# Reordering the opening of a fused dynamic-convolution and maxout kernel: two products in halves, and w1 cast by GpSimd's transfers

## The chip, the cores and the metric

The kernel runs on one core of a Trainium2 chip. The metric is the device time of one execution in microseconds (us); lower is better. Runs of the same kernel differ: the three runs of the kernel before lie between 410.51 and 413.79 us.

## What is computed

A dynamic convolution with seven taps feeds a two-branch maxout layer.

```python
# x: (8, 4160, 192), weight_gen: (8, 4160, 8 heads, 7 taps), float32
w = weight_gen - np.max(weight_gen, axis=-1, keepdims=True)
w = np.exp(w)
w = w / (np.sum(w, axis=-1, keepdims=True) + 1e-09)
x_pad = np.concatenate([np.zeros((B, pad, D), dtype=np.float32), x], axis=1)
...
out = np.einsum('bshk,bskhg->bshg', w, x_unf)   # 24 features a head
# then, with tokens = 33280, w1 and w2 (192, 1024), w_out (1024, 192)
h1 = x @ w1
h2 = x @ w2
g = np.maximum(h1, h2)
return (g @ w_out).astype(np.float32)
```

The kernel writes max(h1, h2) as h1 + relu(h2 - h1). So it needs the difference w2 - w1 (called wd) for the hidden layer, and the product w1 · w_out (called w10), which carries the h1 part straight to the result.

## The kernel before, in words

**Tiling.** Each of the 128 partitions holds 260 consecutive tokens, called columns here. Columns are worked in batches of 16; a batch is cut into pieces of 8, and in the first two batches into pieces of 4. For a piece, VectorE multiplies seven shifted copies of x by the softmax weights into m_t (`mul`, L208). In the first two batches TensorE then sums the seven taps and transposes at once (`sum_transpose`, L275), and ScalarE copies the result out as yt; in later batches VectorE adds the taps and a DMA transposes. `hid_tile` (L334) multiplies yt by wd, ScalarE applies Relu (`relu`, L349), `out_first` and `out_second` multiply by w10 and w_out, and `evac` copies the result for its store.

**Order.** The schedule is manual: on every engine instructions run in the order in which the code emits them, and an instruction whose data has not come holds up all behind it on its engine. Transfers issued by SyncE (SP) take one queue, those issued by GpSimd (POOL) another; POOL's loads write float32 inputs as bfloat16. `behind(first, load)` makes POOL wait for a named instruction before it issues a load.

**The opening** is the part in question, L561 to L742.

- SP's queue, in order: the weights of columns 0 to 7 (`load_wg`, L568); into xs the six columns of halo and then four columns of x (L569); the left halves of w1 and w2 for their first 128 rows (ws0E, ws1E; `load_w`, L577); the last 64 rows (ws0T, ws1T; `load_w_rest`, L584); the weights of columns 8 to 15; the right halves of ws0E and ws1E; and the weights of batch 1.
- POOL's queue: x columns 4 to 7 behind the first exponential (L655), columns 8 to 11 behind the first product (L656), 12 to 15, then w_out as wo (L658); later the first half of batch 1 behind the first Relu (L676) with its halo (L154).
- VectorE: the softmax sum and the subtraction for columns 0 to 7 (`red` L178, `shift` L188), two casts of xs (L611), the product of columns 0 to 3 (L612), the left difference of the weights (`w_diff`, L618), the difference of the last rows (L664), the product of columns 4 to 7 (L666), the right difference (L667), the sums for columns 8 to 15 and for batch 1 (L670, L672), the subtraction for columns 8 to 15 (L686), and the product of columns 8 to 11 (L689).
- TensorE: 24 matmuls that only keep it busy (`keep_warm`, L647), the tap sums of columns 0 to 3 with the first `halves_swapped` (L622) between their two halves, the second `halves_swapped`, hidden tiles 0 and 1, the tap sums of columns 4 to 7, and so on. `halves_swapped` makes the copy of wd with its partitions' halves exchanged, which ScalarE writes back into wd (L626); a hidden tile reads both forms.
- ScalarE: exponentials, logarithms and weights, a cast of the left half of ws0E to w1 (L616), the copies of wd and yt, the Relus, and after yt of columns 4 to 7 the casts of ws0T and of the right half of ws0E (L690, L691). `w1_transposed` (L631) needs these; it leads to w1t (L722), `w10_product` (L699, which also reads wo) and w10 (L713, L715).

One tap sum in `sum_transpose` reads blocks of 128 values, in which the two pairs of columns of a piece lie side by side, 64 values each; so it needs the products of both pairs.

Of the kernel before, what the change touches and what calls it, by code (L numbers as in the profile page):

```python
# [13 lines left out]
ALU = mybir.AluOpType  # L14
# [3 lines left out]
def _sub(base: bass.AP, off: int, dims):  # L18
    ap = [list(base.ap[0])] + [[int(s), int(c)] for s, c in dims]
    return dataclasses.replace(base, offset=base.offset + off, ap=ap)  # L20
# [3 lines left out]
def kernel(  # L24
# [9 lines left out]
    nc = tc.nc  # L34

    B, S, D = x.shape
    H, K = weight_gen.shape[2], weight_gen.shape[3]
    F = moe_w1.shape[1]
    P = 128
# [90 lines left out]
    def load_x(b, o, n, halo=True):  # L130

        t, at = x_at(b, o)
        load = nc.gpsimd.dma_start(  # L133
            out=t[:, at + PAD * D:at + (PAD + n) * D],
            in_=bass.AP(tensor=x.tensor, offset=actual(BATCHES[b][0] + o) * D,
                        ap=[[CPP * D, P], [1, n * D]]),
        )
        if 0 < b < NB - 1 and o == 0 and halo:
            load_halo(b)
        if "wrap" in xb_ts and t is xb_ts["wrap"]:  # L140
            nc.gpsimd.memset(t[0:1, 0:PAD * D], 0.0)
            nc.gpsimd.dma_start(
                out=t[1:P, 0:PAD * D],
                in_=bass.AP(tensor=x.tensor, offset=(CPP - PAD) * D, ap=[[CPP * D, P - 1], [1, PAD * D]]),
            )
        return load
# [11 lines left out]
    def exp_sum(b, i=0, of=1):  # L158
        if i == 0:
            e_ts[b] = pe_.tile([P, BATCHES[b][1] * WGC], FP32, name="e_t", tag="e")  # L160
        w = BATCHES[b][1] * WGC // of
        return nc.scalar.activation(out=e_ts[b][:, i * w:(i + 1) * w], in_=wg_ts[b][:, i * w:(i + 1) * w], func=AF.Exp)  # L162
# [15 lines left out]
    def red(b, i=0, of=1):  # L178
        hs, at, ap = part(b, i, of)
        nc.vector.reduce_sum(out=sums(b, hs), in_=_sub(e_ts[b], at, ap), axis=AX.X)  # L180
# [27 lines left out]
    def mul(b, o):  # L208

        n = dict(pieces(b))[o]  # L210
        t, at = x_at(b, o)
        if n == 4 and b < 2:
            m_out = _sub(m_t, K * o * D, [[64, 2], [P, K * 6], [1, 64]])
            x_in = _sub(t, at, [[2 * D, 2], [D, K], [1, 2 * D]])
        else:
            m_out = m_t[:, K * o * D:K * (o + n) * D]
            x_in = _sub(t, at, [[D, K], [1, n * D]])
        return nc.vector.tensor_tensor(  # L218
            out=m_out, in0=x_in,
            in1=_sub(en_ts[b], o * WGC * 2, [[2, K * n * H], [0, G // 2], [1, 2]]),  # L220
            op=ALU.mult,
        )

# [45 lines left out]
    def half(j):  # L269
        return slice(64 * j, 64 * j + 64)  # L270
# [4 lines left out]
    def sum_transpose(u, taps=range(K), amid=lambda: None, now=True):  # L275

        b, o, n = UNITS[u]
        assert n == 4
        yps = ps["r" if "r" in ps else "o"].tile([P, 1024], FP32, name="yps", tag="op")
        for k in range(6):  # L280
            if k == 3:
                amid()
            for t in taps:
                for r in range(2):
                    at = (K * o + t * n) * D + k * P
                    nc.tensor.matmul(  # L286
                        yps[:, r * 512 + k * 64:r * 512 + (k + 1) * 64],
                        lhsT=m_t[half(r), at:at + P], rhs=ident[half(r), half(r)],
                        start=(k == 0 and t == taps[0]), stop=(t == taps[-1]),
                        skip_group_check=True,  # L290
                    )
        def copy():
            yt = pyt.tile([P, 8 // 2 * 3 * P], BF16, name="yt", tag="yt")
            yt_of[u] = nc.scalar.copy(out=_sub(yt, 0, [[64, 2], [P, 6], [1, 64]]),  # L294
                                      in_=_sub(yps, 0, [[512, 2], [64, 6], [1, 64]]))
            yt_ts[u] = yt

        if now:
            copy()
        return copy  # L300
# [4 lines left out]
    def behind(first, load):  # L305

        tc.add_manual_dep(load.ins, first.ins.name, SYNC, reason="its place among the transfers")
# [26 lines left out]
    def hid_tile(t):  # L334


        u = TILES[t][0]
        fs, w = chunks(t)
        for f in fs:
            for s in range(3):  # L340
                for j in range(2):
                    nc.tensor.matmul(  # L342
                        hid_out(t, f, j), lhsT=wd_at(j, s, f // 4, f % 4 * P, P),
                        rhs=_sub(yt_ts[u][half(j), :], (s + j) % 3 * P, [[3 * P, w // P], [1, P]]),
                        start=(f == fs[0] and s == 0), stop=(f == fs[-1] and s == 2),
                        skip_group_check=True,
                    )

    def relu(rd, t0, n):  # L349

        (hd, at), k = hd_at[t0], rd_at[t0][1]
        relu_of[t0] = nc.scalar.activation(out=rd[:, k * 1024:(k + n) * 1024], in_=hd[:, at:at + n * 1024],  # L352
                                           func=AF.Relu)
# [126 lines left out]
    def room(g):  # L480

        t0, n = GROUPS[g]
        if "c" in ps:
            ab = ps["ab"].tile([P, 2048], FP32, name="hd2", tag="ab")
            for t in range(t0, t0 + n - 1):
                hd_at[t] = ab, (t - t0) * 1024
            hd_at[t0 + n - 1] = ps["c"].tile([P, 1024], FP32, name="hd1", tag="c"), 0
        else:
            for t in range(t0, t0 + n):
                hd_at[t] = ps["h"].tile([P, 1024], FP32, name="hdp", tag="hd"), 0  # L490
        rd = prd.tile([P, 3 * 1024], BF16, name="rd_t", tag="rd")
        for t in range(t0, t0 + n):
            rd_at[t] = (rd, t - t0)
        return rd
# [66 lines left out]
    with tc.tile_pool(name="pstage", bufs=1) as pstage:  # L561
# [4 lines left out]

        xb_ts[0] = pxb.tile([P, (16 + PAD) * D], BF16, name="xb_t", tag="xb")
        load_wg(0, nc.sync, 0, 8)  # L568
        for at, c, n in ((0, 2, PAD), (PAD, 8, 4)):  # L569
            nc.sync.dma_start(  # L570
                out=xs[:, at * D:(at + n) * D],
                in_=bass.AP(tensor=x.tensor, offset=c * D, ap=[[CPP * D, P], [1, n * D]]),
            )
# [33 lines left out]
            step(0, 0, 2)  # L607
        weights(0, 0)
        weights(0, 4)
        for at, n in ((0, PAD), (PAD, 4)):  # L610
            nc.vector.tensor_copy(out=xb_ts[0][:, at * D:(at + n) * D], in_=xs[:, at * D:(at + n) * D])  # L611
        first_mul = mul(0, 0)  # L612
        w1 = {kind: pstage.tile([P, w], BF16, name="w1" + kind)
              for kind, w in (("E", F), ("T", HF))}

        nc.scalar.copy(out=w1["E"][:, 0:HF], in_=ws["E", 0][:, 0:HF])  # L616

        def w_diff(kind, c, to):  # L618
            nc.vector.tensor_tensor(out=wd[:, to * HF:(to + 1) * HF], in0=ws[kind, 1][:, c:c + HF],
                                    in1=ws[kind, 0][:, c:c + HF], op=ALU.subtract)  # L620

        def halves_swapped(frm, bank):  # L622

            nc.tensor.matmul(bank, lhsT=ident[:, 64:64 + P], rhs=wd[:, frm * HF:(frm + 1) * HF],
                             start=True, stop=True, skip_group_check=True)
            nc.scalar.copy(out=wd[:, (frm + 3) * HF:(frm + 4) * HF], in_=bank)  # L626
# [20 lines left out]
        def keep_warm(times):  # L647

            for _ in range(times):
                nc.tensor.matmul(warm[:, 0:512], lhsT=ident[:, 0:P], rhs=_sub(ident, 0, [[0, 4], [1, P]]),  # L650
                                 start=True, stop=True, skip_group_check=True)

        keep_warm(24)
        w_diff("E", 0, 0)
        behind(first_exp, load_x(0, 4, 4))  # L655
        behind(first_mul, load_x(0, 8, 4))  # L656
        load_x(0, 12, 4)
        nc.gpsimd.dma_start(  # L658
            out=wo[:, :].rearrange("p (f d) -> p f d", d=D),
            in_=bass.AP(tensor=moe_w_out.tensor, offset=0, ap=[[D, P], [P * D, FCH], [1, D]]),  # L660
        )

        sum_transpose(0, amid=lambda: halves_swapped(0, warm[:, 512:1024]))
        w_diff("T", 0, 2)  # L664
        halves_swapped(2, warm[:, 0:512])
        mul(0, 4)  # L666
        w_diff("E", HF, 1)  # L667

        exp_sum(0, 1, 2)
        red(0, 1, 2)  # L670
        exp_sum(1)
        red(1)  # L672
        rd = room(0)
        hid_tile(0)
        relu(rd, 0, 1)
        behind(relu_of[0], load_x(1, 0, 8))  # L676
        hid_tile(1)

        def last_rows():
# [1 line left out]
            halves_swapped(1, other[:, 0:512])  # L681

        features = sum_transpose(1, amid=last_rows, now=False)
        ln(0, 1, 2)
        relu(rd, 1, 1)
        shift(0, 1, 2)  # L686
        weights(0, 8)
        features()
        mul(0, 8)  # L689
        nc.scalar.copy(out=w1["T"], in_=ws["T", 0])  # L690
        nc.scalar.copy(out=w1["E"][:, HF:F], in_=ws["E", 0][:, HF:F])  # L691
        hidden(1)
        weights(0, 12)
        ln(1)
        shift(1)
        mul(0, 12)
        tp = w1_transposed()
# [272 lines left out]
```

## Time and profile before

| what | value |
|---|---|
| median of 3 runs | 412.61 us |
| lowest and highest run | 410.51 and 413.79 us |
| the profiled execution | 413.05 us |
| its span in the trace | 411.2 us |
| mean granted TensorE clock | 0.994 |
| TensorE busy | 398.7 us, 97% of the span |
| VectorE, ScalarE, GpSimd busy | 376.0, 357.1 and 74.7 us |

The span is what the trace covers; the profiled execution took 1.85 us more than that outside it. All positions below are us from the start of the span. PE is TensorE's matmul side and PEld its weight loads, DVE is VectorE, ACT ScalarE, POOL GpSimd, SP SyncE. A name with an arrow, such as `m_t<-xb_t,en_t`, is output and inputs; L218 is line 218. Square brackets at the end of a line give the idle time of the engine ahead of it, and what ended that.

### The profile page before, as it was taken

The page shows a single profiled execution, that of the slowest core. Times are in us where ns is not written, and L with a number is a line of the kernel's source. Part 1 is how long each engine was busy: PE and PEld are TensorE (multiplying, and loading weights), DVE is VectorE, ACT ScalarE, POOL GpSimd, SP SyncE. Part 2 cuts the span into 40 slices and gives each one's busy share as a digit, 9 for nine tenths or more (in the row PEclk, how much of TensorE's full clock was granted, in tenths as well). Part 3 has the DMA queues.
Part 4 walks back from the last instruction along what each step waited for, and adds up shares of the span by engine and source line. Part 5 has one row for each costly group of instructions (what it writes and reads, how often), then busy time and mean ns, then how long its engine had stood idle before and what let it go on. Part 6 is the DMA issues. An engine that isn't in the chain of part 4 may idle for free.

```text
span 411.2 us, 16177 instructions
## 1 busy us (share of the span) xinstructions
PE 398.7 (97%) x7411; PEld 316.3 (77%) x7411; DVE 376.0 (91%) x223; ACT 357.1 (87%) x424; POOL 74.7 (18%) x105
## 2 busy tenths in 40 slices
PE   7779999999999999999999999999999999999996
PEld 2568989777777787777777777787778777777795
DVE  4889999999999999999999999999999999999500
ACT  3599989999989999898998899998999989988872
POOL 1202013122220122222202121220132221110000
PEclk9899999999999999999999999999999999999999
DMA  8947396876557874964775498478748647944413
GB/s 234 211 105 176 104 197 160 175 162 148 159 120 152 229 159 110 257 168 87 227 201 122 93 254 185 79 242 135 175 102 244 167 70 222 193 97 120 133 73 126
DMA packets 63062, 65.53 MB, mean 159 GB/s; under 512 B 47761, under 2 KB 52113, under 8 KB 62992
## 3 DMA queue, kind: packets, MB, share of 16 engines
q1 hardware_dynamic: 54320, 40.15, 35.7%
q0 software_dynamic: 8528, 24.23, 29.4%
q8 instruction: 58, 0.95, 0.9%
q10 hardware_dynamic: 144, 0.10, 0.1%
q14 instruction: 12, 0.10, 0.1%
HBM read 36.55 MB, written 25.56 MB: 151 GB/s over the span
## 4 chain that ended last, share of the span: by engine, by line
PE 91%; ACT 5%; DMA 2%; DVE 1%; issue 0%; SPq 0%; ACTq 0%; DVEq 0%
PE op_ps L382 41%; PE hd L342 38%; PE op_ps L394 8%; ACT rd_t L352 2%; PE hdp L342 2%; DMA xs<-in_x_dram 2%; PE yps L286 2%; DVE m_t L218 1%; ACT en_t L202 1%; ACT yt L294 1%; ACT w1t L722 0%; ACT xb_t L150 0%; ACT o_t L438 0%; ACT wd L626 0%; DVE xb_t L611 0%
## 5 line engine op out<-in xcount | busy, mean ns | idle before, releaser
L352 ACT ACTIVATE rd_t<-hd 128x1024 bf16<-128x1024 f32 (+1 forms) x206 | 234.5, 1187 | 26.6 <-PE hd L342 25.3
L382 PE MATMUL op_ps<-wo,rd_t 64*128 64x192 bf16 x4160 | 210.3, 243 | 0.4 <-issue 0.3
L382 PEld LDWEIGHTS <-rd_t 64*128 64x128 bf16 x4160 | 180.3, 94 | 16.6 <-issue 0.6
L218 DVE TENSOR_TENSOR m_t<-xb_t,en_t 128x10752 bf16<-128x10752 bf16 (+1 forms) x37 | 187.5, 5070 | 1.2 <-ACT en_t L202 1.1
L342 PE MATMUL hd<-yt,wd 64*128 64x512 bf16 (+1 forms) x1584 | 187.3, 360 | 0.3 <-issue 0.3
L342 PEld LDWEIGHTS <-wd 64*128 64x128 bf16 x1776 | 93.0, 94 | 44.3 <-issue 2.7
L260 POOL CAST gate<-yt 128x1 f32<-128x1 bf16 x29 | 37.2, 1284 | 261.4 <-DMA yt<-y_t 261.4
L234 DVE TENSOR_TENSOR m_t<-m_t 128x4608 bf16<-128x4608 bf16 (+1 forms) x30 | 74.1, 2470 | 0.1
L438 ACT COPY o_t<-op_ps 128x384 f32<-128x384 f32 (+1 forms) x99 | 57.4, 590 | 12.6 <-PE op_ps L382 12.5
L394 PE MATMUL op_ps<-w,yt 64*128 64x192 bf16 x780 | 55.3, 243 | 0.5 <-ACT w L715 0.4
L394 PEld LDWEIGHTS <-yt 64*128 64x128 bf16 x780 | 38.1, 94 | 17.1 <-issue 1.7
L240 DVE TENSOR_TENSOR m_t<-m_t 128x3072 bf16<-128x3072 bf16 (+1 forms) x29 | 49.9, 1722 | 0.1
L202 ACT ACTIVATE en_t<-wg_t 128x896 bf16<-128x896 f32 (+2 forms) x45 | 36.0, 823 | 0.7 <-DVE wg_t L191 0.7
L243 DVE TENSOR_TENSOR y_t<-m_t 128x1536 bf16<-128x1536 bf16 (+1 forms) x29 | 27.3, 940 | 0.5
L133 POOL DMA_DIRECT2D xb_t<-in_x_dram x34 | 18.2, 536 | 32.5 <-ACT rd_t L352 20.7
L191 DVE TENSOR_TENSOR wg_t<-wg_t,ln_t 128x280 f32<-128x280 f32 (+5 forms) x46 | 22.1, 480 | 2.0 <-ACT ln_t L186 2.0
L162 ACT ACTIVATE e_t<-wg_t 128x896 f32<-128x896 f32 (+2 forms) x18 | 16.2, 902 | 1.5 <-DMA wg_t<-in_weight_gen_dram 1.5
L180 DVE TENSOR_REDUCE s_rest<-e_t 128x64 f32<-128x448 f32 (+2 forms) x27 | 16.3, 602 | 0.3 <-ACT e_t L162 0.3
L352 ACT ACTIVATE rd_t<-hdp 128x1024 bf16<-128x1024 f32 x16 | 16.1, 1059 | 0.4 <-PE hdp L342 0.4
L342 PE MATMUL hdp<-yt,wd 64*128 64x256 bf16 x192 | 14.0, 281 | 1.0 <-ACT rd_t L352 0.6
L286 PE MATMUL yps<-ident,m_t 64*128 64x64 bf16 x636 | 11.3, 191 | 2.7 <-DVE m_t L218 2.7
L286 PEld LDWEIGHTS <-m_t 64*128 64x128 bf16 x636 | 10.6, 96 | 3.8 <-DVE m_t L218 3.2
(53 smaller groups left out, 73.6 us busy)
## 6 DMA issues: line engine op xcount, KB each, us to landing
out_dram<-o_t SPq DMA_DIRECT2D x22, 768.0 KB, 5.1
xb_t<-in_x_dram POOLq DMA_DIRECT2D x30, 384.0 KB, 5.2
out_dram<-o_t SPq DMA_DIRECT2D x20, 384.0 KB, 3.1
wg_t<-in_weight_gen_dram POOLq DMA_DIRECT2D x13, 448.0 KB, 5.7
xb_t<-xb_t POOLq DMA_DIRECT2D x15, 288.0 KB, 5.3
xb_t<-in_x_dram POOLq DMA_DIRECT2D x4, 192.0 KB, 5.1
xs<-in_x_dram SPq DMA_DIRECT2D x1, 576.0 KB, 4.5
ws0E<-in_moe_w_dram SPq DMA_DIRECT2D x2, 256.0 KB, 6.8
```

Source lines behind the costliest of these rows:

```text
L202: nc.scalar.activation(out=_sub(en_ts[b], (o * WGC + j * N * K) * 2, [[2 * N, K], [2, N], [1, 2]]), in_=_sub(wg_ts[b], (o * H + j * N) * K ...
L218: return nc.vector.tensor_tensor(out=m_out, in0=x_in, in1=_sub(en_ts[b], o * WGC * 2, [[2, K * n * H], [0, G // 2], [1, 2]]), op=ALU.mult,)
L234: nc.vector.tensor_tensor(out=taps(0, 1, 3), in0=taps(0, 1, 3), in1=taps(3, 1, 3), op=ALU.add)
L240: nc.vector.tensor_tensor(out=taps(0, 2, 2), in0=taps(0, 2, 2), in1=taps(1, 5, 2), op=ALU.add)
L243: nc.vector.tensor_tensor(out=_sub(y_ts[b], o * D, [[64, 2], [P, 3 * w // 2], [1, 64]]), in0=taps(0, 1, 1), in1=taps(2, 1, 1), op=ALU.add,)
L260: nc.gpsimd.tensor_copy(out=gate, in_=yt[:, 0:1])
L286: nc.tensor.matmul(yps[:, r * 512 + k * 64:r * 512 + (k + 1) * 64], lhsT=m_t[half(r), at:at + P], rhs=ident[half(r), half(r)], start=(k == ...
L342: nc.tensor.matmul(hid_out(t, f, j), lhsT=wd_at(j, s, f // 4, f % 4 * P, P), rhs=_sub(yt_ts[u][half(j), :], (s + j) % 3 * P, [[3 * P, w // ...
L352: relu_of[t0] = nc.scalar.activation(out=rd[:, k * 1024:(k + n) * 1024], in_=hd[:, at:at + n * 1024], func=AF.Relu)
L382: return nc.tensor.matmul(op_out(c), lhsT=rd[half(r), k * 1024 + at:k * 1024 + at + P], rhs=wo[half(r), f * D:(f + 1) * D], start=False, s ...
L394: nc.tensor.matmul(op_out(c + j), lhsT=yt_ts[u][half(j), (3 * i + (s + j) % 3) * P:(3 * i + (s + j) % 3 + 1) * P], rhs=w10[half(j), s * D: ...
L438: nc.scalar.copy(out=_sub(o, c % 24 * D, [[D, len(qs)], [h * D, 2], [1, D]]), in_=_sub(tile_, at + (qs[0] - p) * D, [[D, len(qs)], [512, 2 ...
```

## The change

Four things change, all in the opening.

1. xs comes in three transfers instead of two (halo, two columns, two columns). The casts and the product of columns 0 to 3 become: cast the halo, cast two columns, product of the first pair of columns, cast two columns, product of the second pair. A new helper `mul_pair` multiplies one pair of a piece.
2. VectorE's order becomes: left difference, first pair of columns 4 to 7, difference of the last rows, second pair, sums of columns 8 to 15, right difference, subtraction for columns 8 to 15, sums of batch 1, product of columns 8 to 11. ScalarE does the exponential of columns 8 to 15 ahead of the second copy of wd, their logarithm right behind the first Relu, their weights ahead of the second Relu, and the logarithm of batch 1 ahead of the third.
3. ScalarE's three casts of w1 go. POOL issues three casting transfers of w1 in the place where it issued wo; wo follows behind the first Relu, after x of batch 1 and its halo.
4. `keep_warm` makes 22 matmuls instead of 24.

```diff
+    def mul_pair(b, o, j):
+
+        t, at = x_at(b, o)
+        return nc.vector.tensor_tensor(
+            out=_sub(m_t, K * o * D + 64 * j, [[P, K * 6], [1, 64]]),
+            in0=_sub(t, at + 2 * j * D, [[D, K], [1, 2 * D]]),
+            in1=_sub(en_ts[b], (o + 2 * j) * WGC * 2, [[2, K * 2 * H], [0, G // 2], [1, 2]]),
+            op=ALU.mult,
+        )
...
-        for at, c, n in ((0, 2, PAD), (PAD, 8, 4)):
+        for at, c, n in ((0, 2, PAD), (PAD, 8, 2), (PAD + 2, 10, 2)):
...
-        for at, n in ((0, PAD), (PAD, 4)):
-            nc.vector.tensor_copy(out=xb_ts[0][:, at * D:(at + n) * D], in_=xs[:, at * D:(at + n) * D])
-        first_mul = mul(0, 0)
+        for j, parts in enumerate((((0, PAD), (PAD, 2)), ((PAD + 2, 2),))):
+            for at, n in parts:
+                nc.vector.tensor_copy(out=xb_ts[0][:, at * D:(at + n) * D], in_=xs[:, at * D:(at + n) * D])
+            first_mul = mul_pair(0, 0, j)
...
-        nc.scalar.copy(out=w1["E"][:, 0:HF], in_=ws["E", 0][:, 0:HF])
...
-        keep_warm(24)
+        keep_warm(22)
         w_diff("E", 0, 0)
         behind(first_exp, load_x(0, 4, 4))
         behind(first_mul, load_x(0, 8, 4))
         load_x(0, 12, 4)
+        nc.gpsimd.dma_start(out=w1["E"], in_=bass.AP(tensor=moe_w1.tensor, offset=0, ap=[[F, P], [1, F]]))
+        for h in range(2):
+            nc.gpsimd.dma_start(out=w1["T"][half(h), :], in_=bass.AP(
+                tensor=moe_w1.tensor, offset=P * F + h * HF, ap=[[F, 64], [1, HF]]))
+        mul_pair(0, 4, 0)
+        sum_transpose(0, amid=lambda: halves_swapped(0, warm[:, 512:1024]))
+        exp_sum(0, 1, 2)
+        w_diff("T", 0, 2)
+        halves_swapped(2, warm[:, 0:512])
+        mul_pair(0, 4, 1)
+        red(0, 1, 2)
+        w_diff("E", HF, 1)
+
+        exp_sum(1)
+        rd = room(0)
+        hid_tile(0)
+        relu(rd, 0, 1)
+        behind(relu_of[0], load_x(1, 0, 8))
         nc.gpsimd.dma_start(
             out=wo[:, :].rearrange("p (f d) -> p f d", d=D),
             in_=bass.AP(tensor=moe_w_out.tensor, offset=0, ap=[[D, P], [P * D, FCH], [1, D]]),
         )
-
-        sum_transpose(0, amid=lambda: halves_swapped(0, warm[:, 512:1024]))
-        w_diff("T", 0, 2)
-        halves_swapped(2, warm[:, 0:512])
-        mul(0, 4)
-        w_diff("E", HF, 1)
-
-        exp_sum(0, 1, 2)
-        red(0, 1, 2)
-        exp_sum(1)
-        red(1)
-        rd = room(0)
-        hid_tile(0)
-        relu(rd, 0, 1)
-        behind(relu_of[0], load_x(1, 0, 8))
+        ln(0, 1, 2)
+        shift(0, 1, 2)
         hid_tile(1)
...
         features = sum_transpose(1, amid=last_rows, now=False)
-        ln(0, 1, 2)
+        weights(0, 8)
+        red(1)
+        mul(0, 8)
         relu(rd, 1, 1)
-        shift(0, 1, 2)
-        weights(0, 8)
         features()
-        mul(0, 8)
-        nc.scalar.copy(out=w1["T"], in_=ws["T", 0])
-        nc.scalar.copy(out=w1["E"][:, HF:F], in_=ws["E", 0][:, HF:F])
+        ln(1)
         hidden(1)
         weights(0, 12)
-        ln(1)
         shift(1)
         mul(0, 12)
```

## The prediction, made before the change was run

> **What bounds the kernel now.** I read the page first: TensorE is the bound over the whole span, so only what moves the start of its unbroken work counts.
>
> ```profile
> span 411.2 us, 16177 instructions
> PE 398.7 (97%) x7411; PEld 316.3 (77%) x7411; DVE 376.0 (91%) x223; ACT 357.1 (87%) x424; POOL 74.7 (18%) x105
> ```
>
> TensorE is idle for 12.5 us in all. Its own timeline puts most of the gaps ahead of 32 us; from 32 us its work is nearly unbroken. What the change moves ends before that. So I read the chain of waits of the first 60 us (start, us, what).
>
> ```profile
> 1.69 6.92 DMA xs<-in_x_dram
> 9.29 2.97 DVE m_t L218
> 14.39 0.81 ACT yt L294
> 15.24 2.46 PE hdp L342 x22
> 21.68 0.52 ACT w1T L690
> 22.20 0.52 ACT w1E L691
> 22.72 1.84 ACT rd_t L352 x2
> 25.34 1.83 ACT rd_t L352 x2
> ```
>
> The reader is to see three stretches: a transfer, the first product, and then ScalarE, link by link from 19.5 to 33 us. The casts of w1 (0.52 + 0.52) lie on that last stretch. Next the timeline from 10 to 24 us: what each step waited for.
>
> ```profile
> 12.16 0.69 DVE L619 TENSOR_TENSOR wd<-ws1E,ws0E 128x512 bf16<-128x512 f32 x1
> 13.57 0.69 DVE L619 TENSOR_TENSOR wd<-ws1T,ws0T 128x512 bf16<-128x512 f32 x1 [0.72 <-DMA ws1T<-in_moe_w_dram]
> 14.18 2.96 DVE L218 TENSOR_TENSOR m_t<-xb_t,en_t 128x5376 bf16<-128x5376 bf16 x1
> 15.08 0.59 ACT L626 CAST wd<-warm 128x512 bf16<-128x512 f32 x1
> 15.73 1.77 PEld L342 LDWEIGHTS <-wd 64*128 64x128 bf16 x21 [0.38 <-ACT wd L626]
> 16.35 0.95 ACT L162 ACTIVATE e_t<-wg_t 128x896 f32<-128x896 f32 x1 [0.20 <-DMA wg_t<-in_weight_gen_dram]
> 17.21 1.00 ACT L352 ACTIVATE rd_t<-hdp 128x1024 bf16<-128x1024 f32 x1
> 18.75 0.58 ACT L626 CAST wd<-other 128x512 bf16<-128x512 f32 x1 [0.54 <-PE other L624]
> ```
>
> Here the first product is not alone: the hidden tiles wait for the second copy of wd (15.08 to 15.67), which goes back to the landing of ws1T at 13.5, and the first Relu (17.21) follows an exponential that waited for batch 1's weights until 16.3. Transfers, not products, set both. The DMA view, asked for the issues of short windows, gives each landing (KB, us from issue):
>
> ```profile
> xb_t<-in_x_dram POOLq DMA_DIRECT2D x1, 192.0 KB, 9.0
> wg_t<-in_weight_gen_dram SPq DMA_DIRECT2D x1, 448.0 KB, 5.4
> wo<-in_moe_w_out_dram POOLq DMA_DIRECT2D x1, 384.0 KB, 7.2
> ```
>
> The first is x of columns 4 to 7: issued at 4.24, landed at 13.24. Last, the windows view of the first hidden tiles; its columns are the stretch, five engines' busy time, the granted clock, the DMA share and GB/s.
>
> ```profile
> 12.00:13.50 1.50, 1.19 (x53) 0.92 (x55) 0.85 (x2) 0.05 (x1) 0.94 (x2) 1.00 1.05 353
> 13.50:15.00 1.50, 1.43 (x43) 0.89 (x38) 1.43 (x2) 1.15 (x2) 1.02 (x2) 0.58 1.05 260
> 15.00:16.50 1.50, 1.26 (x11) 0.68 (x12) 1.50 (x1) 1.30 (x4) 0.00 (x0) 0.50 1.08 197
> 16.50:18.00 1.50, 1.50 (x48) 1.22 (x43) 1.50 (x3) 1.50 (x2) 0.00 (x0) 0.78 1.06 124
> ```
>
> All 16 DMA engines are full (share above 1), and the clock was halved from 13.9 to 17.3, after TensorE had idled for 2.7 us from 9.6.
>
> **The change part by part.** As marker I take the start of the fifth Relu: 25.21 before. From there to w10 the order on ScalarE is unchanged, so what the marker gains or loses, the end does.
>
> *The first product in halves.* The halo lands at 5.72 as before and its cast ends at 6.53. xs's columns landed at 8.6; the first two now land between 6.6 (right behind the halo) and 8.0; I take 7.2, the middle by bytes. Products of 5376 and 10752 elements take 2.96 and 5.75, so one of 2688 takes 0.17 + 1.39 = 1.56. Casts of 1152 and 768 take 0.76 and 0.56, so one of 384 takes 0.36. First pair 7.55 to 9.1, second cast 9.0 to 9.4, second pair to 10.9, where the product ended at 12.25: 1.3 earlier (0.5 with a landing at 8.0). SP issues one transfer more (0.42); its later issues already waited (8.62, 9.74, 10.89, each just after an earlier landing), so I cost it at nothing, covered by the full DMA engines; uncovered it costs 0.4.
>
> *Columns 4 to 7 ahead of the last rows' difference.* The left difference follows at 10.9 to 11.5. Then the first pair of columns 4 to 7 needs the x that landed at 13.24. In the kernel before that was hidden, as its product stood at 14.18; now VectorE stands still for 1.7 us, and behind that pair the difference of the last rows, which had its data at 13.5, starts at 13.3 + 1.5 = 14.8 instead of 13.57. The second `halves_swapped` runs at 15.5 and its copy ends at about 16.65 instead of 15.67: hidden tiles wait 1.0 longer. Bounds for that landing: loads of the same size from the same queue took 4.6 and 5.1 at 12.6 and 13.1, which would put it at 9; then the difference stays at ws1T's 13.5, and the tiles go on at 15.3. I take 9.0, its own row, as its issue and what runs ahead of it do not change.
>
> *ScalarE's order.* The second copy of wd ends at 16.65, batch 1's exponential runs 16.65 to 17.5, the first Relu from 17.55 (17.21 before). The hidden tiles' last 21 matmuls, then 42 tap sums and `halves_swapped` 1 take 1.15 + 0.7 + 0.35 at full clock and 2.25 + 0.95 + 0.6 at half. So the third copy of wd starts at 19.0 or at 20.5. From there to the marker only sums of steps: copy 0.5, weights 0.6, Relu 0.92, yt 0.69, logarithm 0.2, two Relus 1.85, weights 0.6 = 5.36. The marker comes at 24.35 or 25.9. The removed casts (1.04) are in this: before, the same way from 18.75 took 6.46.
>
> *The clock.* A stretch at half clock lasted 3.4 us and began 4.3 us after a 2.7 us gap began. The new gap, from 13.0 to 15.5, is as long; the critical matmuls run 16.7 to 20.5. Whether the stretch covers them all depends on where it falls; I take half, marker 25.1. The Trainium skill, "TensorE: Matmul & The Clock Gate", Part 1, says that the clock falls after at least one whole idle window of about 3.4 us and that the windows run free of the kernel. The row here fell after 2.7 us of idleness, so the measurement decides against the first half; by the rule the sum would be the full-clock marker.
>
> *w1 by POOL.* ScalarE's first cast (9.74, 0.62) stood in idle time, worth nothing. POOL now issues five loads behind the first product, at about 11 to 13.7; the last three are 384 KB in bf16 as wo was, with wo's 7.2 landing by 20.9, needed by the transposes that stood at 21.22 and 22.77. The loads start 1.3 earlier and share the DMA engines with batch 1's weights: these land between 16.3 and 17.0 (half of 1.3 more). The copy of wd covers that up to 16.65; beyond, 0.35 at most. wo now follows x of batch 1 and its halo, at about 19.7; the halo landed at 25.8, and wo's bytes stood in the queue for 3.3 us behind nothing, so it lands between 26.9 (7.2) and 29.1 (25.8 + 3.3). `w10_product` started at 28.6; ScalarE takes its result at 30.6, the product takes 1.5. So wo may come as late as 29.1 at no cost; then each us costs one.
>
> *keep_warm.* Two matmuls fewer at full clock, 0.4 us sooner idle: off the path except through the clock.
>
> **Sum.** 25.1 against 25.21: -0.1. On the profiled execution, 411.2 of span and 1.85 around it, that gives 412.95. It stands 0.44 above the median shown, so for the median I say 412.5.
>
> **The rivals.**
> 1. *The x of columns 4 to 7 comes in time.* Then nothing waits for it, the first Relu stands at 17.21 behind batch 1's weights (16.3 + 0.86), and the way from there is Relu 0.92, logarithm 0.2, and the 5.36: 23.7, or 24.0 with a little half clock. That is -1.3: 411.3. For it: in the trace's packet records 14 of the 16 engines had finished that load by 11.1, only two came at 12.4 and 12.8. Against: a load counts when its last engine has come.
> 2. *TensorE stays at full clock.* Marker 24.35, -0.85: 411.7. Against it stands the halved clock after a gap of this length. This is what the rule named above gives.
> 3. *wo comes too late*: slower. It sits behind two transfers in POOL's queue, and POOL itself stands behind the first Relu and the landing of columns 12 to 15. If it lands at 30.5, the w10 product starts 1.4 past its slack: 414.0. It decides from 29.1 on. Against: between 24 and 28.5 the DMA share is below 0.1, so the lane is free.
>
> That the change does not do what it says is excluded for ScalarE, where three instructions are simply gone; for the halves it is rival 1 turned round: they finish early for nothing.
>
> **How the numbers follow.** My forecast 0.47, with a range of its own of 411.6 to 413.4 (full to half clock: -0.85 to +0.7, on 412.6). Rival 1 0.25, rival 2 0.12, rival 3 0.12, something unseen 0.04. The range takes in rivals 1 to 3 and about 1 us by which a median of three can stray (the runs shown spread by 3.3): 410.2 to 414.2. About 1% (4.1 us) is what a measurement of this kernel can tell from no change. Every case lies within it: same 0.88. Faster 0.05 and slower 0.07 are the unseen, a stray median and the far end of rival 3.
>
> **What would show it.** In the profile after: the second pair of columns 0 to 3 ends near 10.9; the first pair of columns 4 to 7 waits for xb_t until about 13.2; the difference of the last rows starts near 14.8; the first Relu at 17.5; no w1 cast on ScalarE; the fifth Relu near 25.1; `w10_product` does not wait for wo. I am wrong if the fifth Relu stands more than 1 us from 25.1, if the marker's move does not reach the end, or if a transpose waits for w1.

## The result, and the profile after

The changed kernel takes 410.25 us (median of 20 runs, 408.74 to 411.71), the kernel before 411.87 us in the same comparison (20 runs, 410.16 to 414.21). The ratio is 0.9962 with a 95% interval of 0.9944 to 0.9980: some 1.6 us, 0.4%, faster, and well inside 1%. The profiled execution took 411.41 us, its span is 409.5 us. Both profiled executions had a stretch at half clock (mean clock 0.994 before, 0.989 after), so the two traces are of one kind, though the stretch was twice as long after.

| position in the trace, us | before | after |
|---|---|---|
| last columns of xs landed | 8.6 | 6.7 |
| product of columns 0 to 3 ended | 12.25 | 10.2 |
| x of columns 4 to 7 landed | 13.2 | 11.0 |
| weights of batch 1 landed | 16.3 | 14.8 |
| first Relu began | 17.21 | 15.85 |
| third copy of wd began | 18.75 | 18.66 |
| fifth Relu (the marker) began | 25.21 | 23.93 |
| first matmul with w10 began | 31.84 | 30.56 |
| 14th copy of a result began | 84.42 | 82.81 |
| span | 411.2 | 409.5 |

From the 14th copy on the two traces keep their distance. The gain is there at the first Relu (1.36), is down to 0.09 at the third copy of wd, and is back at the marker (1.28), because the way there no longer holds the two casts. Another 0.3 comes between 31 and 84 us.

The chain of waits of the first 60 us, after (start, us, what). Lines of the changed kernel have other numbers: L635 is the cast back into wd, L362 the Relu, L352 the hidden tiles, L296 the tap sums, L227 `mul_pair`, L628 `w_diff`, L304 yt.

```profile
1.23 4.35 DMA xs<-in_x_dram
5.59 6.09 DMA ws1T<-in_moe_w_dram
13.92 0.59 ACT wd L635
14.56 2.37 PE hdp L352 x16
16.93 1.28 PE yps L296 x32
18.66 0.59 ACT wd L635
21.65 1.83 ACT rd_t L362 x2
```

The product of columns 0 to 3 is no longer a link; a transfer of weights takes its place. It landed at 11.68, but the difference that needs it began at 12.54, because VectorE was still at the first pair of columns 4 to 7, which had begun at 11.06, when its x was there. So that x holds this chain too. The two casts of w1 are gone from ScalarE's stretch, but TensorE links stand in it, between 14.6 and 18.6 us. The timeline of the same stretch:

```profile
8.66 1.56 DVE L227 TENSOR_TENSOR m_t<-xb_t,en_t 128x2688 bf16<-128x2688 bf16 x1
11.06 1.56 DVE L227 TENSOR_TENSOR m_t<-xb_t,en_t 128x2688 bf16<-128x2688 bf16 x1 [0.23 <-DMA xb_t<-in_x_dram]
12.54 0.69 DVE L628 TENSOR_TENSOR wd<-ws1T,ws0T 128x512 bf16<-128x512 f32 x1
14.81 0.95 ACT L162 ACTIVATE e_t<-wg_t 128x896 f32<-128x896 f32 x1 [0.30 <-DMA wg_t<-in_weight_gen_dram]
15.85 1.02 ACT L362 ACTIVATE rd_t<-hdp 128x1024 bf16<-128x1024 f32 x1
18.66 0.59 ACT L635 CAST wd<-other 128x512 bf16<-128x512 f32 x1 [1.64 <-PE other L633]
```

The reader is to see that VectorE's wait for x is there, as foreseen, but 0.23 long and not 1.7; and that ScalarE now waits 1.64 for TensorE ahead of the third copy of wd. Why TensorE is late shows in the windows (stretch; busy time of PE, PEld, DVE, ACT and POOL, each with its number of instructions; granted clock, DMA share, GB/s):

```profile
10.50:12.00 1.50, 1.50 (x73) 1.22 (x67) 1.26 (x2) 0.57 (x1) 1.46 (x3) 0.85 1.06 303
12.00:13.50 1.50, 0.70 (x19) 0.42 (x13) 1.50 (x3) 0.99 (x3) 1.18 (x3) 0.50 1.05 393
13.50:15.00 1.50, 1.36 (x10) 0.44 (x11) 1.50 (x2) 1.07 (x3) 0.00 (x0) 0.50 1.17 248
15.00:16.50 1.50, 1.50 (x18) 1.04 (x16) 0.82 (x2) 1.41 (x2) 0.00 (x0) 0.50 1.11 201
16.50:18.00 1.50, 1.50 (x47) 1.43 (x43) 0.95 (x2) 0.52 (x2) 0.71 (x2) 0.50 0.81 137
```

The clock was halved for 6.8 us, from 11.5 to 18.4 (3.4 us before, from 13.7 to 17.2), all over the hidden tiles and the second tap sums. And the DMA view of after, asked for the same issues as before (KB, us from issue to landing):

```profile
xb_t<-in_x_dram POOLq DMA_DIRECT2D x1, 192.0 KB, 6.8
wg_t<-in_weight_gen_dram SPq DMA_DIRECT2D x1, 448.0 KB, 5.8
wo<-in_moe_w_out_dram POOLq DMA_DIRECT2D x1, 384.0 KB, 7.6
```

x of columns 4 to 7, issued at 4.18, took 6.8 and not 9.0; batch 1's weights took no shorter but were issued at 9.00 instead of 10.89; wo, issued at 18.39, landed at 26.0, ahead of its use at 27.33.

### The profile page after: what moved, and what is told of

It is laid out like the page before. It is cut to its first block, busy times and chain, and to the rows that moved or that the text cites. A ratio compares the mean times of both kernels' runs of the same rounds, so it can differ in the third digit from the quotient of the medians.

```text
span 409.5 us, 16186 instructions
## 1 busy us (share of the span) xinstructions
PE 398.4 (97%) x7409; PEld 317.4 (77%) x7409; DVE 376.3 (92%) x226; ACT 355.4 (87%) x421; POOL 78.0 (19%) x108
## 4 chain that ended last, share of the span: by engine, by line
PE 91%; ACT 5%; DMA 3%; issue 0%; DVE 0%; SPq 0%; ACTq 0%; DVEq 0%
PE op_ps L392 41%; PE hd L352 39%; PE op_ps L404 8%; ACT rd_t L362 2%; PE hdp L352 2%; DMA ws1T<-in_moe_w_dram 1%; PE yps L296 1%; DMA xs<-in_x_dram 1%; ACT en_t L202 1%; ACT w1t L733 0%; ACT yt L304 0%; ACT xb_t L150 0%; ACT wd L635 0%; ACT o_t L448 0%; DVE wd L628 0%
## 5 line engine op out<-in xcount | busy, mean ns | idle before, releaser
L362 ACT ACTIVATE rd_t<-hd 128x1024 bf16<-128x1024 f32 (+1 forms) x206 | 234.5, 1187 | 26.0 <-PE hd L352 24.7
L392 PEld LDWEIGHTS <-rd_t 64*128 64x128 bf16 x4160 | 180.5, 94 | 16.1 <-ACTq L425 0.3
L352 PE MATMUL hd<-yt,wd 64*128 64x512 bf16 (+1 forms) x1584 | 187.5, 360 | 0.0
L218 DVE TENSOR_TENSOR m_t<-xb_t,en_t 128x10752 bf16<-128x10752 bf16 (+1 forms) x35 | 181.7, 5191 | 2.6 <-ACT en_t L202 2.6
L352 PEld LDWEIGHTS <-wd 64*128 64x128 bf16 x1776 | 93.8, 94 | 44.1 <-issue 2.8
L270 POOL CAST gate<-yt 128x1 f32<-128x1 bf16 x29 | 38.9, 1342 | 260.3 <-DMA yt<-y_t 260.3
L133 POOL DMA_DIRECT2D xb_t<-in_x_dram x34 | 18.2, 536 | 29.2 <-ACT rd_t L362 15.9
L362 ACT ACTIVATE rd_t<-hdp 128x1024 bf16<-128x1024 f32 x16 | 16.1, 1048 | 0.5 <-PE hdp L352 0.4
L352 PE MATMUL hdp<-yt,wd 64*128 64x256 bf16 x192 | 14.7, 287 | 1.3 <-ACT rd_t L362 1.0
L296 PE MATMUL yps<-ident,m_t 64*128 64x64 bf16 x636 | 12.1, 195 | 2.2 <-DVE m_t L227 2.2
L296 PEld LDWEIGHTS <-m_t 64*128 64x128 bf16 x636 | 11.4, 98 | 3.5 <-DVE m_t L227 2.7
```

Source lines behind the costliest of these rows:

```text
L218: return nc.vector.tensor_tensor(out=m_out, in0=x_in, in1=_sub(en_ts[b], o * WGC * 2, [[2, K * n * H], [0, G // 2], [1, 2]]), op=ALU.mult,)
L270: nc.gpsimd.tensor_copy(out=gate, in_=yt[:, 0:1])
L296: nc.tensor.matmul(yps[:, r * 512 + k * 64:r * 512 + (k + 1) * 64], lhsT=m_t[half(r), at:at + P], rhs=ident[half(r), half(r)], start=(k == ...
L352: nc.tensor.matmul(hid_out(t, f, j), lhsT=wd_at(j, s, f // 4, f % 4 * P, P), rhs=_sub(yt_ts[u][half(j), :], (s + j) % 3 * P, [[3 * P, w // ...
L392: return nc.tensor.matmul(op_out(c), lhsT=rd[half(r), k * 1024 + at:k * 1024 + at + P], rhs=wo[half(r), f * D:(f + 1) * D], start=False, s ...
```

## The experiments

Three theories stood after this result. "Transfers": the opening hangs on landings, and three transfers of xs move them. "ScalarE": what lasts is the casts taken from ScalarE; the landings of single traces differ by chance. "Order": the new order brings the gain. Ratios are to the kernel before, with 95% intervals.

**The two kernels again, for second traces.** No edit.

> The kernel before, unchanged, for a second trace. Theory 'transfers' (the three transfers of xs let SP's later loads be issued and land 1.5 us sooner, and the first Relu follows batch 1's weights): x of columns 4 to 7 lands about 13.2 again, batch 1's weights at 16.3, the fifth Relu at 25.2. Theory 'ScalarE' (the gain is the casts taken from ScalarE; the landings of the two traces differ by chance): the landings move by 1 us or more between two runs of the same kernel.

> The changed kernel, unchanged, for a second trace. If the landings are chance, x of columns 4 to 7 and batch 1's weights land up to 1.5 us away from 11.0 and 14.8, and the half-clock stretch falls elsewhere; if the three transfers set them, they land within 0.5 of that.

Before again: x landed at 13.0, batch 1's weights at 16.1, first Relu 16.99, marker 24.54, span 411.3. After again: 10.9, 14.7, 15.60, 23.53, and 409.4. Both pairs of landings repeat within 0.3. The half-clock stretch does not: 24.0 to 27.4 instead of 13.7 to 17.2 in the one, 14.3 to 17.7 instead of 11.5 to 18.4 in the other. From the first Relu to the marker it is 7.55 instead of 8.00, and 7.93 instead of 8.08.

**Part 1 alone: three transfers and halves.**

```diff
-        for at, c, n in ((0, 2, PAD), (PAD, 8, 4)):
+        for at, c, n in ((0, 2, PAD), (PAD, 8, 2), (PAD + 2, 10, 2)):
...
-        first_mul = mul(0, 0)
+            first_mul = mul_pair(0, 0, j)
```

> The kernel before with part 1 alone: three transfers of xs, and the product of columns 0 to 3 in two halves. 'Transfers': first Relu near 15.9 instead of 17.2, fifth Relu near 23.9, about 1.3 us (0.3%) faster. 'ScalarE': first Relu 17.2, fifth 25.2, no change.

Ratio 0.9999 (0.9981 to 1.0018). First Relu 15.28, marker 22.85, 2.4 earlier than before and 1.7 earlier than before again. So the opening moved as "transfers" has it, and yet the median did not: neither theory. The trace itself ends at 410.3, 0.9 ahead of before, so 1.5 of the 2.4 went between the marker and the end: 0.4 ahead of the first matmul with w10, with a half-clock stretch from 22.6 to 26.0, and 1.1 behind it. TensorE's timeline of this kernel shows where most of the 1.1 went:

```profile
39.06 0.67 PE L392 MATMUL op_ps<-wo,rd_t 64*128 64x192 bf16 x12 [0.45 <-issue]
44.16 0.50 PE L352 MATMUL hdp<-yt,wd 64*128 64x256 bf16 x6 [0.53 <-issue]
47.89 0.67 PE L392 MATMUL op_ps<-wo,rd_t 64*128 64x192 bf16 x12 [0.28 <-issue]
51.62 1.27 PE L352 MATMUL hd<-yt,wd 64*128 64x256 bf16 x20 [0.30 <-issue]
```

Four gaps, 1.56 in all, in the midst of runs of matmuls that wait for no engine. The trace's packet records hold, on the queue of kind "instruction", a packet of 16 KB that ends 1.3 to 1.5 ahead of each gap's end (37.8, 42.8, 46.6, 50.2). In the other traces every such gap ends 1.2 to 1.5 behind such a packet too, though most of these packets are followed by no gap. I read the gaps as TensorE waiting for its code; that rests on the two following each other in time. The gaps also account for the length of this way. From the first matmul with w10 to the 14th result copy the kernel before takes 52.6 with gaps of 0.64, before again 53.1 with 0.75, this one 53.7 with 1.56, after 52.25 and after again 51.9 with none: without the gaps 51.9 to 52.3.

**Three transfers, the product whole.** The three transfers are those of the diff above; the casts follow them:

```diff
-        for at, n in ((0, PAD), (PAD, 4)):
+        for at, n in ((0, PAD), (PAD, 2), (PAD + 2, 2)):
...
         first_mul = mul(0, 0)
```

> The kernel before with xs in three transfers and three casts, the product of columns 0 to 3 whole. 'Transfers': as with the halves, first Relu near 15.9, 0.3% faster. 'Halves' (it is the earlier product that counts): first Relu 17.2, no change. 'ScalarE': no change.

Ratio 0.9985 (0.9966 to 1.0004). First Relu 16.01, 1.2 earlier, with a whole product that ended at 10.8: so most of the 1.9 that part 1 alone gave is there without the halves. But this trace had the clock halved from 11.8 to 18.6, the third copy of wd came at 18.86, and the marker at 25.32, later than before.

**Part 3 alone: w1 by POOL.**

```diff
-        nc.scalar.copy(out=w1["E"][:, 0:HF], in_=ws["E", 0][:, 0:HF])
...
+        nc.gpsimd.dma_start(out=w1["E"], in_=bass.AP(tensor=moe_w1.tensor, offset=0, ap=[[F, P], [1, F]]))
...
-        nc.scalar.copy(out=w1["T"], in_=ws["T", 0])
-        nc.scalar.copy(out=w1["E"][:, HF:F], in_=ws["E", 0][:, HF:F])
```

> The kernel before with part 3 alone: no casts of w1 on ScalarE, POOL's three casting transfers in wo's place, wo behind the halo of batch 1. 'ScalarE': fifth Relu at 24.2 (25.2 less 1.04), 0.25% faster. 'Transfers': the added 384 KB and the moved wo cost as much at the first Relu or at the w10 product as the casts give: fifth Relu between 24.2 and 25.2, first Relu 17.2 or later.

Ratio 0.9979 (0.9960 to 0.9999). From the first Relu to the marker 6.46, where before again took 7.55: the two casts' 1.04 and little else. First Relu at 16.15 and marker at 22.61 with two transfers of xs, at a clock that was full throughout the opening.

**Part 1 undone in the changed kernel.** The diff of part 1 the other way round; columns 4 to 7 stay in two pairs.

> The changed kernel with part 1 undone: xs in two transfers, columns 0 to 3 in one product; the new order and w1 by POOL stay. Theory 'ScalarE' (what lasts of the gain is the casts taken from ScalarE; landings differ by chance and are given back later): as the changed kernel, ratio to before 0.996 to 0.998. Theory 'transfers': the gain goes, ratio near 1.000.

Ratio 1.0002 (0.9973 to 1.0032). By the ratio this speaks for "transfers", though the interval still overlaps the changed kernel's. The trace does not: x landed at 11.1 and batch 1's weights at 14.4 with only two transfers, so the landings of before (13.2, 13.0) are not what two transfers always give, and the marker stood at 24.05, 0.12 behind the changed kernel's.

**Part 3 undone in the changed kernel.** w1's casts back on ScalarE, wo back in its place.

> The changed kernel with part 3 undone: ScalarE casts w1 (three casts, as before) and POOL issues wo in its old place; halves and new order stay. 'ScalarE': the gain goes, ratio 0.999 to 1.001. Theory 'order' (the logarithm and weights moved ahead of the Relus bring it): the gain stays, 0.996 to 0.998.

Ratio 1.0003 (0.9978 to 1.0029): the gain is gone, as "ScalarE" has it, and against "order" (its interval and the changed kernel's just touch). Its trace also prices the half clock. The landings were nearly the changed kernel's (x at 11.2, batch 1's weights at 14.9), the steps of ScalarE up to here are the same, and the clock was full throughout the opening:

```profile
16.89 0.58 ACT L637 CAST wd<-other 128x512 bf16<-128x512 f32 x1
```

This third copy of wd has no wait ahead of it and begins 1.10 behind the first Relu; in the changed kernel it was 2.81, at 18.66. So the half clock took some 1.7 there.

**Part 2 undone: old order with parts 1 and 3.** `keep_warm` is back at 24, too.

> The kernel before with parts 1 and 3: halves, and w1 by POOL, in the old order on VectorE and ScalarE. 'ScalarE': the gain stays, 0.996 to 0.998, fifth Relu 1.0 us earlier counted from the first Relu (7.0 instead of 8.0). 'Order': no gain.

Ratio 0.9958 (0.9937 to 0.9979), first Relu 15.24, marker 21.71, 6.47 between them. The new order is worth nothing that shows in the time: all of the gain is there without it. The difference of the last rows, which here stands ahead of columns 4 to 7, began at 11.52 and not at 12.54, and the second copy of wd at 12.82 and not at 13.92. The w10 product waited here:

```profile
25.32 1.48 PE L716 MATMUL pw<-wo,w1t 128*128 128x192 bf16 x16 [0.77 <-DMA wo<-in_moe_w_out_dram]
```

**TensorE kept busy.**

```diff
-        keep_warm(22)
+        keep_warm(25)
...
         w_diff("T", 0, 2)
+        keep_warm(4)
         halves_swapped(2, warm[:, 0:512])
```

> The changed kernel with 25 matmuls instead of 22 at the start, and 4 more just ahead of the second halves_swapped, where TensorE waits for VectorE. Theory 'clock' (in the new order TensorE idles there, its clock is halved over the hidden tiles and the second tap sums, and this eats what the casts give): the half-clock stretch shrinks or leaves the hidden tiles, the way from the first Relu to the first matmul with w10 falls from 14.6 to about 13.3 us, ratio to before 0.993 to 0.995. Theory 'order' (the new order itself makes that way long): 14.6 stays, ratio 0.996.

From the first Relu (0.6 later here, at 16.43, with x landing at 12.0) to the first matmul with w10 13.25, not 14.7, and the clock stays full:

```profile
13.50:15.00 1.50, 0.70 (x4) 0.11 (x3) 1.50 (x3) 0.38 (x2) 0.00 (x0) 1.00 1.12 273
15.00:16.50 1.50, 1.15 (x23) 1.04 (x25) 1.50 (x3) 1.22 (x3) 0.00 (x0) 1.00 1.16 213
16.50:18.00 1.50, 1.50 (x76) 1.22 (x72) 0.72 (x2) 1.39 (x4) 0.27 (x1) 1.00 0.92 158
```

The theory "clock" holds for that stretch. The ratio is 0.9962 (0.9938 to 0.9985), not below 0.995: the median is 410.05, against the changed kernel's 410.25. Each run lists its mean clock, and these say why. In all nine runs here it is 0.998 or more, and they lie between 408.89 and 410.73. The changed kernel's runs at 0.998 or more (11 of 20) have a median of 409.71, those at 0.995 or less (7) 411.25; before, in the 81 runs beside these experiments, 411.13 (38) and 412.94 (30). So a half-clock stretch costs 1.5 to 1.8 when it comes, and it comes in about a third of the runs of both kernels. With TensorE kept busy no run had one; the fastest runs did not become faster.

**x of columns 4 to 7 late.** `weights` returns its last instruction for this.

```diff
-        weights(0, 4)
+        late = weights(0, 4)
...
-        behind(first_exp, load_x(0, 4, 4))
+        behind(late, load_x(0, 4, 4))
```

> The changed kernel with the load of x of columns 4 to 7 issued 2.7 us later, behind the weights of columns 4 to 7. By the step of the prediction that failed: the first pair of columns 4 to 7 waits until about 13.5 on VectorE, the difference of the last rows starts at about 15, the first Relu at 17.3 or later, and all of the gain goes (ratio 0.999 to 1.002). If the wait is hidden by batch 1's weights: first Relu by 16.2, ratio 0.996 to 0.997.

Ratio 1.0061 (1.0038 to 1.0085): all of the gain goes and more. In all four runs the mean clock was 0.993 or less, and in the trace the half-clock stretch lasted 10.2, from 11.5 to 21.7. VectorE's and ScalarE's timelines:

```profile
13.91 1.56 DVE L228 TENSOR_TENSOR m_t<-xb_t,en_t 128x2688 bf16<-128x2688 bf16 x1 [3.18 <-DMA xb_t<-in_x_dram]
15.38 0.68 DVE L629 TENSOR_TENSOR wd<-ws1T,ws0T 128x512 bf16<-128x512 f32 x1
16.77 0.59 ACT L636 CAST wd<-warm 128x512 bf16<-128x512 f32 x1 [3.13 <-PE warm L634]
18.69 1.02 ACT L363 ACTIVATE rd_t<-hdp 128x1024 bf16<-128x1024 f32 x1 [0.49 <-PE hdp L353]
```

The first pair comes 2.85 later than in the changed kernel, the difference of the last rows 2.84, the first Relu 2.84, the marker 2.99, the span 2.9. So the chain that I forecast from this landing is right, link by link and one for one.

**The first Relu ahead of batch 1's exponential,** in the kernel with parts 1 and 3 and the old order.

```diff
-        exp_sum(1)
-        red(1)
         rd = room(0)
         hid_tile(0)
         relu(rd, 0, 1)
+        exp_sum(1)
+        red(1)
```

> Halves and w1 by POOL in the old order, with the exponential and the sums of batch 1 moved behind the first Relu. Theory 'transfers' (the first Relu stands behind that exponential, and so behind the landing of batch 1's weights): first Relu at about 14.3 instead of 15.2, first matmul with w10 0.5 to 0.9 us earlier, ratio to before 0.993 to 0.995. If the hidden tiles are what the Relu waits for: first Relu 15.0 to 15.3, ratio 0.996.

And the same with wo moved up:

```diff
+        nc.gpsimd.dma_start(
+            out=wo[:, :].rearrange("p (f d) -> p f d", d=D),
...
         behind(relu_of[0], load_x(1, 0, 8))
-        nc.gpsimd.dma_start(
-            out=wo[:, :].rearrange("p (f d) -> p f d", d=D),
...
```

> As e11, with wo issued right behind w1, ahead of x of batch 1. Rival 3 of the prediction (wo comes late) for the fast opening: in the kernel with the old order, halves and w1 by POOL the w10 product waited 0.8 us for wo; here it does not, the first matmul with w10 comes 0.2 to 0.8 us earlier than in e11. If nothing hangs on wo: as e11.

The first Relu came at 14.12: it does stand behind that exponential, and so behind batch 1's weights. But the first matmul with w10 only moved from 28.35 to 28.16, and the ratio is 0.9963 (0.9949 to 0.9978). The w10 product waits for wo:

```profile
25.32 1.48 PE L716 MATMUL pw<-wo,w1t 128*128 128x192 bf16 x16 [0.94 <-DMA wo<-in_moe_w_out_dram]
```

With wo issued right behind w1 (at 13.0 instead of 18.2) that wait is gone, replaced by one for w1t:

```profile
25.68 1.48 PE L716 MATMUL pw<-wo,w1t 128*128 128x192 bf16 x16 [0.55 <-ACT w1t L734]
```

Ratio 0.9957 (0.9941 to 0.9972), the lowest of all, but by their intervals none of the three kernels in the old order with parts 1 and 3 can be told from the changed kernel. In its trace the difference of the last rows waited until 12.09 for ws1T (11.16 in the run before), so the first matmul with w10 stood at 28.91.

## Why the prediction was right, and where not

The forecast was 412.5, no change; it came to 410.25. "No change" as I meant it, less than 1%, holds. The rest holds less well. 410.25 lies 0.05 above the low end of the whole range (410.2) and below the range of my own sum, 411.6 to 413.4 (its terms, -0.85 and +0.7 on 412.6, give 411.75 to 413.3). And the marker stood at 23.93, 1.17 from 25.1, where I had named 1 us as the sign of being wrong; the other two signs did not come (the marker's move reached the end, and no transpose waited for w1). So the way I put first is not what happened. Rival 1 (x in time, 411.3) was nearer, and its marker of 23.7 to 24.0 was met, but by luck: the first Relu came at 15.85 and not at its 17.21, and the half clock then took 1.7 back. By the prediction's steps:

- *The landing of x of columns 4 to 7* is the step that failed. I took 9.0 from its own row and bounded it by 4.6 (the second of the two loads that I set beside it took 5.7, not 5.1); it took 6.8, and 6.2 to 7.7 in the eight other traces with three transfers and this load in its place. The row was one of a scatter: with two transfers 9.0, 8.7, 8.1 and 6.8. VectorE's wait, which I took at 1.7 with 1.0 of it on the path, was 0.23. Rival 1 got 0.25 on the ground of the packet records, which had 14 of 16 engines done by 11.1; that was the better witness. In that one trace the last engine came 1.7 behind the 14th, in no other more than 1.0.
- *One more transfer on SP's queue* I costed at nothing, with batch 1's weights landing at 16.3 to 17.0. This term has the wrong sign in the traces: xs's last columns landed at 6.7 instead of 8.6, and SP's later loads, each issued just after an earlier landing, went out at 6.75, 7.99 and 9.00 instead of 8.62, 9.74 and 10.89. So batch 1's weights, behind which the first Relu stands, landed at 14.8. In nine traces with three transfers x of columns 4 to 7 in its old place landed at 11.0 on average (10.5 to 12.0), in four with two at 12.5 (11.1 to 13.2). How much is the split and how much is chance stays open: one kernel with two transfers landed as early as those with three.
- *The product in halves* ended at 10.2 (10.9 foreseen), half products at 1.56 as worked out. Little hangs on it: with the product whole the first Relu came at 16.01, against 15.28 with the halves in the same old order, and xs landed 0.7 later there.
- *ScalarE's order*: the way from the third copy of wd to the marker was 5.27 (5.36 foreseen). The copy stood at 18.66; at full clock and nearly these landings it came at 16.89, with w1's casts back on ScalarE. I had the price of the half clock about right (0 to 1.55; some 1.7 measured) and let it hit half; it hit all, for twice as long as in the row (which is 13.7 to 17.2 in the windows, where I read 13.9 to 17.3). The rule that the clock falls after a whole idle window (the Trainium skill, "TensorE: Matmul & The Clock Gate", Part 1) would have kept it full; here the clock fell after a gap of 2.2. In three other traces (before again, after again, part 1 alone) the longest gap in the 3.4 us ahead of the stretch was 1.2. That the windows run free of the kernel agrees: in two runs of the kernel before the stretch began at 13.7 and at 24.0.
- *w1 by POOL*: w1 landed by 19.2, needed at 21.57; wo at 26.0 (26.9 to 29.1 foreseen), and nothing waited for it. Rival 3 is real only where the opening is faster still: wo was waited for 0.8 to 0.9 in the kernels that reach the w10 product at 25.3.

So of the four parts the casts give a gain that shows: with halves and the old order 0.9958 against 0.9999 without them, and 0.9962 against 1.0003 in the new order. Part 1 adds where they are gone (0.9962 against 1.0002, 0.9958 against 0.9979; the intervals overlap), nothing alone. The new order adds nothing that shows.

These ratios hold a second thing: how many of a version's runs had a half-clock stretch. Here runs are sorted as above (mean clock 0.998 or more, 0.995 or less), with the number of runs in brackets and those between left out; beside them stands the kernel before in the same series (medians, us):

| version | full clock | before, full | half clock | before, half |
|---|---|---|---|---|
| part 1 alone | 411.26 (3) | 411.61 (11) | 412.42 (8) | 412.60 (13) |
| three transfers, product whole | 411.06 (5) | 411.61 (11) | 411.97 (7) | 412.60 (13) |
| part 3 alone | 410.92 (7) | 411.61 (11) | 411.76 (4) | 412.60 (13) |
| part 1 undone | 410.72 (2) | 411.00 (16) | 412.09 (7) | 413.25 (10) |
| part 3 undone | 411.64 (6) | 411.00 (16) | 413.06 (3) | 413.25 (10) |
| parts 1 and 3, old order | 410.08 (11) | 411.00 (16) | 409.88 (1) | 413.25 (10) |

At like clock the casts still count. Part 1 alone and part 1 undone lie 0.2 to 1.2 ahead of the kernel before, on few runs; so their ratios of 1.000 seem to come in part from many half-clock runs, 8 and 7 of 12. The three kernels in the old order with parts 1 and 3 had 3 such runs in 34, the changed kernel 7 in 20. Whether that is the order, the two matmuls of `keep_warm` (part 4 was not run alone) or chance is not shown. In the one trace of part 1 alone, gaps that I read as waits for code took 0.9 more than before; that they always do was not tried, as no kernel here changes the code's loading alone.

## What to carry to other kernels

When a step is moved behind a landing, take that landing from several traces, or from the packets, before pricing the wait: one row of a saturated queue was off by 2 us, and everything in order behind it follows one for one. Look at what a moved gain meets next (a halved clock, a code load, a transfer that had slack); here each could take some 1 us back. Sort runs by their granted clock before reading a difference of half a per cent.

## What the runs showed that was not expected

The half-clock stretch lasts 3.4, 6.8 or, in one trace, 10.2 us, falls between 11 and 28 us at a place that differs from run to run, and accounts for a good part of the spread of the times: 1.5 us between the medians of the changed kernel's runs with and without it, 1.8 for the kernel before. Gaps of TensorE that follow a 16 KB packet on the instruction queue took 0.2 to 0.6 each between 38 and 64 us, up to 1.56 in one trace, and there was none of 0.2 in any of four traces in the new order with parts 1 and 3 (the changed kernel's two, the one kept busy and the one with late x).
